# Three fused layers on one core: weight conversion in fewer steps, paced differently, and decay tables widened on GpSimd

## The chip, the cores and the metric

The kernel runs on one NeuronCore of one Trainium2 chip. The metric is the device time of one execution in microseconds. Engines are named PE (TensorE matmul), DVE (VectorE), ACT (ScalarE), POOL (GpSimd) and SP (SyncE, whose queue issues the DMAs).

## What is computed

Three layers follow one another, each on the output of the one before:

```python
# 1. retention: q, k, v are (batch 4, heads 8, seq 576, dim 64)
ret = (q @ k.T / 8) * Dmat          # Dmat[i, j] = gamma_h ** (i - j) for i >= j, else 0
x = ret @ v                         # reshaped to (2304, 512)
# 2. feed-forward, w_in (512, 2048), w_out (2048, 512)
h = x @ w_in
x = (h * clip(h + 3, 0, 6) / 6) @ w_out
# 3. feed-forward, w_in (512, 1024), w_out (1024, 512)
h = x @ w_in
solu = h * softmax(h)
ln = (solu - mean) / sqrt(var + 1e-6) * g_ln
out = ln @ w_out
```

The four weight matrices arrive as 64-bit floats (each as two 32-bit words). The retention inputs arrive as 32-bit floats.

## The kernel before, in words

**Matmuls in three passes.** For the two feed-forward layers every operand is held as a sum of two parts, hi and lo, that PE's fp32r format can hold. A product is three matmuls: hi by hi, hi by lo, lo by hi (`mlp_h`, `mlp_x2`, `mm_h2`, `mm_out`).

**Weight conversion.** `Weights.split` turns one half-tile of 128 x 512 64-bit weights (512 KB, tile `wraw`, two buffers) into hi and lo. It builds the 32-bit value from the two words. First ACT scales the upper word read as a float (L119, into `wz`). Then DVE shifts it left by three bits (L122, into `wt`), puts the sign bit back (L123), masks out the exponent (L124), multiplies the lower word by it (L125) and adds both (L128). Then ACT rounds the sum to hi (L130) and DVE subtracts hi to get lo (L132; every third time on POOL). L125 is the last reader of `wraw`: the next load into that buffer waits for it. There are 48 conversions: 12 during the retention, 20 in the first feed-forward layer, 16 for the last layer's weights (these have lines L134 and L135 for half of them).

**Pacing.** The retention runs over 16 pairs of heads (`attention`), three steps `s` to a pair. PE's program order for pair n is: scores s(n), chunk states u(n), values xp(n-1), last scores z(n), values from the states xp(n-1). DVE does the masked copy `st` (L334), the states (L350), `st4` (L361) and the scaled result `xa` (L387). From step W_FROM = 5 on, two of three steps also call `wq.step()`, which converts one half-tile: steps 5, 6, 8, 9, 11, 12, 14, 15, 17, 18, 20, 21. From pair A_FROM = 5 on, each step also issues two pieces of the first feed-forward layer (`mlp_a`). That layer's second matmuls (`mlp_x2`) begin at step 27 and need conversions 6 to 11.

**Queues.** All bulk DMAs are issued in program order by SP. An instruction in SP's queue that waits (a `wraw` load for its buffer, say) holds up everything behind it. A scheduler sets the order on each engine. What is given below is the order that it made.

**Decay tables.** One DMA (`decay`, 128 x 524) brings four 128-column tables and twelve columns of factors. ACT copies the tables into four tables of 576 columns (`tab_sb`, L442, 20 copies), which `xa` reads.

Of the kernel before, what the change touches and what calls it, by code (L numbers as in the profile page):

```python
# [26 lines left out]
N_DEC = 128 * (H // 2) + H + H // 2  # L27
# [9 lines left out]
W_LOAD = 4  # L37
W_FROM = 5
# [20 lines left out]
def retention_hardswish_solu_kernel(ctx, tc, kt, qt, kn, vt, w1, w2i, w2o, gln, decay, out):  # L59
# [29 lines left out]
    class Weights:  # L89
# [22 lines left out]
        def split(self, raw, w, scale=None, done=None):  # L112


            z = p0.tile([128, 512], F32, tag="wz", bufs=2, name="wz")
            t = p0.tile([128, 512], I32, tag="wt", bufs=2, name="wt")
            zi, f = z.bitcast(I32), t.bitcast(F32)

            first = se.activation(out=z, in_=raw[:, :, 1].bitcast(F32), func=ACTF.Copy, scale=2.0 ** -112)  # L119
# [168 lines left out]
    def load_pair(pr):  # L288
# [50 lines left out]
    def chunk_states(pr):  # L339
# [379 lines left out]
```

## Time and profile before

| | |
|---|---|
| median of 3 runs | 715.96 us (714.98 to 716.06) |
| profiled execution, its own time | 715.41 us |
| its span in the trace | 713.7 us |
| PE busy | 680.6 us, 95% |
| DVE busy | 441.9 us, 62% |
| ACT busy | 307.2 us, 43% |
| POOL busy | 249.1 us, 35% |
| mean granted TensorE clock | 0.978 |

The first two lines are device times. The span is the stretch that the trace covers; the profiled execution took 1.7 us more than its span. PE's share of busy time is an average over stages with different limits, so it doesn't say by itself which engine a stage waits for. A table by stretches does: each of its rows gives, for a stretch of the span, each engine's busy time with its count of instructions, the granted clock, and how busy the DMA engines were.

### The profile page before, as it was taken

How to read it: one execution, taken by the hardware profiler on the slowest of the kernel's cores; microseconds unless marked ns; L12 is line 12 of the kernel's file. 1: busy time of each engine (PE TensorE's matmuls, PEld its weight loads, DVE VectorE, ACT ScalarE, POOL GpSimd, SP SyncE). 2: the span in 40 equal slices, each digit the busy share in tenths (PEclk: the TensorE clock that was granted, in tenths of full speed). 3: DMA queues.
4: the chain of work that ended last, by engine and by line, in shares of the span. 5: the costliest groups of instructions: out<-in, count | busy, mean ns of one | idle time of the engine just before them, and what ended most of it. 6: DMA issues, size and time to landing. Idle time of an engine off the chain costs nothing.

```text
span 713.7 us, 10518 instructions
## 1 busy us (share of the span) xinstructions
PE 680.6 (95%) x3968; PEld 560.5 (79%) x3968; DVE 441.9 (62%) x673; ACT 307.2 (43%) x536; POOL 249.1 (35%) x233
## 2 busy tenths in 40 slices
PE   7577899999998999999999999999999999999998
PEld 5565677788886997778778888889988888888887
DVE  3899943240496387925777785411178877776780
ACT  4335442342544435433524524413247555454453
POOL 2233341240533133353633502422236633331333
PEclk8789999999999999999999999999999999999999
DMA  9676666113151533315568365013655643233233
GB/s 332 230 227 206 202 191 197 58 45 74 59 192 45 178 110 100 116 56 181 179 198 272 125 228 180 29 45 130 251 166 133 148 89 74 69 80 74 60 82 81
DMA packets 76259, 97.96 MB, mean 137 GB/s; under 512 B 42672, under 2 KB 44976, under 8 KB 75184
## 3 DMA queue, kind: packets, MB, share of 16 engines
q1 hardware_dynamic: 76208, 97.29, 45.1%
q8 instruction: 31, 0.51, 0.3%
q14 instruction: 20, 0.16, 0.1%
HBM read 63.71 MB, written 24.12 MB: 123 GB/s over the span
## 4 chain that ended last, share of the span: by engine, by line
PE 70%; DVE 12%; DMA 7%; issue 5%; ACT 3%; POOL 1%; SPq 0%; DVEq 0%; POOLq 0%; ACTq 0%
PE h L189 17%; PE x L210 16%; PE o L625 14%; PE h L559 14%; DMA wraw<-in_w_dram 6%; PE acc L210 4%; PE xp L286 3%; DVE wt L122 2%; DVE wt L123 2%; DVE wz L125 2%; ACT wz L119 1%; DVE wt L128 1%; PE s L286 1%; DVE wz L124 1%; PE u L286 1%
## 5 line engine op out<-in xcount | busy, mean ns | idle before, releaser
L204 POOL TENSOR_TENSOR g<-gf,g 128x512 fp32r<-128x512 f32 (+1 forms) x80 | 101.4, 1269 | 218.4 <-ACT g L203 194.7
L210 PE MATMUL x<-g,w 128*128 128x512 f32 x648 | 154.6, 393 | 3.0 <-DVE gf L200 1.5
L210 PEld LDWEIGHTS x<-g,w 128*128 128x128 f32 x648 | 120.0, 188 | 31.1 <-DVE gf L200 2.2
L189 PE MATMUL h<-xb,w 128*128 128x512 f32 (+1 forms) x600 | 137.3, 366 | 3.9 <-ACT w L130 2.4
L189 PEld LDWEIGHTS h<-xb,w 128*128 128x128 f32 x600 | 101.8, 193 | 22.4 <-ACT w L130 2.8
L200 DVE SCALAR_TENSOR_TENSOR gf<-r,h 128x512 f32<-128x512 f32 (+1 forms) x80 | 50.3, 629 | 87.2 <-ACT r L199 70.0
L559 PE MATMUL h<-w2i,x2b 128*128 128x512 f32 x432 | 102.0, 389 | 0.0
L625 PE MATMUL o<-w2o,lt 128*128 128x512 f32 (+1 forms) x456 | 101.0, 378 | 0.0
L625 PEld LDWEIGHTS o<-w2o,lt 128*128 128x128 f32 x456 | 82.5, 188 | 16.0
L559 PEld LDWEIGHTS h<-w2i,x2b 128*128 128x128 f32 x432 | 80.6, 188 | 16.3
L189 PE MATMUL h<-xB,w 128*128 128x512 f32 x360 | 82.4, 389 | 0.0
L180 POOL TENSOR_TENSOR lt<-lT,lt 128x512 fp32r<-128x512 f32 x36 | 46.3, 1305 | 93.8 <-ACT lt L179 93.8
L189 PEld LDWEIGHTS h<-xB,w 128*128 128x128 f32 x360 | 67.6, 188 | 14.0
L203 ACT ACTIVATE g<-gf 128x512 fp32r<-128x512 f32 (+1 forms) x80 | 46.9, 587 | 64.3 <-DVE gf L200 64.2
L199 ACT ACTIVATE r<-h,half 128x512 f32<-128x512 f32 (+1 forms) x80 | 50.7, 636 | 40.1 <-PE h L189 39.8
L210 PE MATMUL acc<-g,w 128*128 128x256 f32 (+1 forms) x312 | 63.8, 328 | 0.7 <-ACT x2p L262 0.5
L122 DVE TENSOR_SCALAR wt<-wz 128x512 int32<-128x512 int32 x48 | 33.4, 695 | 39.4 <-ACT wz L119 39.0
L210 PEld LDWEIGHTS acc<-g,w 128*128 128x128 f32 x312 | 50.5, 191 | 8.3 <-POOL g L204 1.0
L180 POOL TENSOR_TENSOR xb<-xa,xb 128x512 fp32r<-128x512 f32 (+7 forms) x32 | 29.1, 927 | 59.9 <-ACT xb L179 59.9
L128 DVE TENSOR_TENSOR wt<-wt,wz 128x512 f32<-128x512 f32 x48 | 44.8, 934 | 0.6
L119 ACT ACTIVATE wz<-wraw 128x512 f32<-128x512 f32 x48 | 31.5, 662 | 26.7 <-DMA wraw<-in_w_dram 21.4
L130 ACT ACTIVATE w<-wt 128x512 fp32r<-128x512 f32 x32 | 20.2, 631 | 45.0 <-DVE wt L128 45.0
(77 smaller groups left out, 744.1 us busy)
## 6 DMA issues: line engine op xcount, KB each, us to landing
wraw<-in_w_dram SPq DMA_DIRECT2D x32, 512.0 KB, 4.2
rv<-in_vt_dram SPq DMA_DIRECT2D x16, 320.0 KB, 4.7
x2l<-x2s SPq DMA_DIRECT2D x18, 256.0 KB, 5.0
out_dram<-osb SPq DMA_DIRECT2D x17, 256.0 KB, 2.0
x2s<-x2p SPq DMA_DIRECT2D x16, 256.0 KB, 3.7
wraw<-in_w2i_dram SPq DMA_DIRECT2D x8, 512.0 KB, 5.7
w2is<-wsi SPq DMA_DIRECT2D x8, 512.0 KB, 4.2
wraw<-in_w2o_dram SPq DMA_DIRECT2D x8, 512.0 KB, 4.8
```

Of the source, the lines that this page charges most:

```text
L119: first = se.activation(out=z, in_=raw[:, :, 1].bitcast(F32), func=ACTF.Copy, scale=2.0 ** -112)
L122: ve.tensor_scalar(out=t, in0=zi, scalar1=3, scalar2=None, op0=ALU.logical_shift_left)
L128: ve.tensor_tensor(out=f, in0=f, in1=z, op=ALU.add)
L180: ge.tensor_tensor(out=x[:, 1, c], in0=src, in1=f32(x[:, 0, c]), op=ALU.subtract)
L189: nc.tensor.matmul(hp, w1t[ff][:, a, c], xb[t, p][:, b, :n], start=(p == 0 and i == 0), stop=(p == NP - 1 and i == 2),)
L199: se.activation(out=r, in_=hp, func=ACTF.Relu, scale=1.0 / 6.0, bias=half)
L200: ve.scalar_tensor_tensor(out=gf, in0=r, scalar=1.0, in1=hp, op0=ALU.min, op1=ALU.mult)
L203: se.activation(out=g[ff][:, 0], in_=gf, func=ACTF.Copy)
L204: ge.tensor_tensor(out=g[ff][:, 1], in0=gf, in1=f32(g[ff][:, 0]), op=ALU.subtract)
L210: nc.tensor.matmul(acc, w1t[ff][:, a, c], g[:, b], start=(first and i == 0), stop=(last and i == 2))
L559: nc.tensor.matmul(h[:, m], x[:, a, c], w[:, b, m * 512:(m + 1) * 512], start=(d == 0 and j == 0), stop=(d == NP - 1 and j == 2),)
L625: nc.tensor.matmul(op, lt[:, a, ff % 4], w[:, b, c:c + n], start=(ff == 0 and j == 0), stop=(ff == NFF2 - 1 and j == 2),)
```

## The change

Three edits.

**Conversion.** L119's copy becomes a two-slope activation (`Prelu`): negative inputs are multiplied by a further 2**32, which shifts their exponent so that the left shift by three brings the sign bit out by itself. The instruction that put the sign back is gone. hi is now made by ACT from the shifted upper word alone, right after the shift, and no longer from the sum. lo is the sum (now written to `wz`) less hi.

**Pacing.** The weight loads begin at step 2 and the conversions at step 4. Up to pair 4 there is one conversion per pair, from pair 5 on two of three steps: steps 4, 7, 10, 13, 16, 17, 19, 20, 22, 23, 25, 26.

**Tables.** The twelve factor columns are a small DMA of their own, now first in SP's queue. The tables (`place`, 128 x 512) follow after pair 0's loads, and POOL widens them in eight copies; ACT's twenty copies are gone.

```diff
-W_LOAD = 4
-W_FROM = 5
+W_LOAD = 2
+W_FROM = 4
...
-            first = se.activation(out=z, in_=raw[:, :, 1].bitcast(F32), func=ACTF.Copy, scale=2.0 ** -112)
+            first = se.activation(
+                out=z, in_=raw[:, :, 1].bitcast(F32), func=ACTF.Prelu, scale=2.0 ** -112, alpha=2.0 ** 32
+            )
...
             ve.tensor_scalar(out=t, in0=zi, scalar1=3, scalar2=None, op0=ALU.logical_shift_left)
-            ve.scalar_tensor_tensor(out=t, in0=zi, scalar=-2 ** 31, in1=t, op0=ALU.bitwise_and, op1=ALU.bitwise_or)
+            se.activation(out=w[:, 0], in_=f, func=ACTF.Copy, scale=1.0 if scale is None else scale)
             ve.tensor_scalar(out=zi, in0=t, scalar1=-2 ** 23, scalar2=None, op0=ALU.bitwise_and)
...
-            ve.tensor_tensor(out=f, in0=f, in1=z, op=ALU.add)
+            ve.tensor_tensor(out=z, in0=f, in1=z, op=ALU.add)
             if scale is None:
-                se.activation(out=w[:, 0], in_=f, func=ACTF.Copy)
                 eng = ge if self.at % 3 == 2 else ve
-                eng.tensor_tensor(out=w[:, 1], in0=f, in1=f32(w[:, 0]), op=ALU.subtract)
+                eng.tensor_tensor(out=w[:, 1], in0=z, in1=f32(w[:, 0]), op=ALU.subtract)
...
-        if pr == 0:
-            nc.sync.dma_start(out=decay_sb, in_=decay)
...
+        if pr == 0:
+            nc.sync.dma_start(out=place_sb, in_=place)
...
+    nc.sync.dma_start(out=decay_sb, in_=decay)
     for pr in range(EARLY):
         load_pair(pr)
...
-        for c in CHUNKS:
-            se.activation(out=tab_sb[p][:, c], in_=decay_sb[:, 128 * p:128 * p + c.stop - c.start], func=ACTF.Copy)
+        ge.tensor_copy(
+            out=tab_sb[p][:, :512].rearrange("p (c q) -> p c q", q=128),
+            in_=place_sb[:, p].unsqueeze(1).to_broadcast([128, 4, 128]),
+        )
+        ge.tensor_copy(out=tab_sb[p][:, 512:], in_=place_sb[:, p, :64])
...
-        if s >= W_FROM and (s - W_FROM) % 3 != 2:
+        if s >= W_FROM and (s - W_FROM) % 3 < (1 if pr < A_FROM else 2):
             wq.step()
```

**What moves on DVE, in pairs 1 and 2.** Names are tile and number; `wt`, `wz` and `w1_0` belong to the first conversion. Before, from the result of pair 0 on:

```order
L387 TENSOR_TENSOR xa0_279<-xp0_251,tab_sb0_96 128x576
L122 TENSOR_SCALAR wt_292<-wz_291 128x512
L123 SCALAR_TENSOR_TENSOR wt_292<-wz_291,wt_292 128x512
L124 TENSOR_SCALAR wz_291<-wt_292 128x512
L334 TENSOR_TENSOR st2_302<-s2_303,mask_100 128x1024
L125 SCALAR_TENSOR_TENSOR wz_291<-wraw_260,wz_291 128x512
L350 SCALAR_TENSOR_TENSOR state2_337<-state2_337,decay_sb_95,u2_336 128x64
L128 TENSOR_TENSOR wt_292<-wt_292,wz_291 128x512
L350 SCALAR_TENSOR_TENSOR state2_337<-state2_337,decay_sb_95,u2_336 128x64 x2
L132 TENSOR_TENSOR w1_0_176<-wt_292,w1_0_176 128x512
```

The same place now, with the new line numbers (L126 the shift, L128 the mask, L129 the product, L132 the sum, L135 lo):

```order
L353 SCALAR_TENSOR_TENSOR state1_232<-state1_232,decay_sb_95,u1_231 128x64 x2
L126 TENSOR_SCALAR wt_257<-wz_256 128x512
L353 SCALAR_TENSOR_TENSOR state1_232<-state1_232,decay_sb_95,u1_231 128x64
L128 TENSOR_SCALAR wz_256<-wt_257 128x512
L129 SCALAR_TENSOR_TENSOR wz_256<-wraw_205,wz_256 128x512
L364 TENSOR_TENSOR st41_266<-z1_265,mask4_102 128x64
L132 TENSOR_TENSOR wz_256<-wt_257,wz_256 128x512
L135 TENSOR_TENSOR w1_0_166<-wz_256,w1_0_166 128x512
L390 TENSOR_TENSOR xa0_280<-xp0_245,tab_sb0_97 128x576
L337 TENSOR_TENSOR st2_291<-s2_292,mask_101 128x1024
```

The first conversion moved from behind `xa0` to ahead of it, into pair 1. One conversion then stands in each pair up to pair 4, always ended before that pair's `xa`.

**What moves in SP's queue.** After pair 2's last load, before:

```order
L309 DMA raw2_126<-in_kn_dram 128x512
L300 DMA rk3_229<-in_kt_dram 128x576
L301 DMA rq3_230<-in_qt_dram 128x576
L308 DMA rv3_234<-in_vt_dram 128x640
L309 DMA rn3_231<-in_kn_dram 128x512
L102 DMA wraw_260<-in_w1_dram 128x1024
```

And now:

```order
L310 DMA raw2_128<-in_kn_dram 128x512
L102 DMA wraw_205<-in_w1_dram 128x1024
L102 DMA wraw_207<-in_w1_dram 128x1024
L303 DMA rk3_223<-in_kt_dram 128x576
L304 DMA rq3_224<-in_qt_dram 128x576
L309 DMA rv3_228<-in_vt_dram 128x640
```

The first two weight loads now stand ahead of pair 3's four loads.

**What moves on PE, in pair 9**, where the second matmuls of the first feed-forward layer begin (`x2_0_0`; `w1_3` and `w1_5` are the weights of conversions 9 and 11). Before:

```order
L210 MATMUL x2_0_0_1047<-g0_3_900,w1_3_179 128x512 x3
L286 MATMUL z9_1094<-rq9_860,rk9_859 64x64 x2
...
L210 MATMUL x2_0_0_1047<-g0_4_955,w1_4_180 128x512 x3
L210 MATMUL x2_0_0_1047<-g0_5_1033,w1_5_181 128x512 x3
L286 MATMUL s10_1127<-rq10_962,rk10_961 128x128 x8
L210 MATMUL x2_0_1_1137<-g0_0_658,w1_0_176 128x512 x3
```

And now:

```order
L212 MATMUL x2_0_0_1025<-g0_3_849,w1_3_169 128x512
L212 MATMUL x2_0_1_1115<-g0_0_607,w1_0_166 128x512 x3
...
L212 MATMUL x2_0_0_1025<-g0_3_849,w1_3_169 128x512 x2
...
L212 MATMUL x2_0_0_1025<-g0_5_1011,w1_5_171 128x512
L212 MATMUL x2_0_1_1115<-g0_3_849,w1_3_169 128x512 x2
L212 MATMUL x2_0_1_1115<-g0_4_915,w1_4_170 128x512 x3
...
L212 MATMUL x2_0_0_1025<-g0_5_1011,w1_5_171 128x512 x2
L289 MATMUL s10_1105<-rq10_922,rk10_921 128x128 x8
```

The matmuls that need lo of conversions 9 and 11 moved back, behind pieces of `x2_0_1`; the rest of PE's order up to pair 9 is as before.

## Rows read from the trace of the kernel before

**Rows 1.** The page: span, busy times, and PE's granted clock in 40 slices.

```profile
span 713.7 us, 10518 instructions
...
PE 680.6 (95%) x3968; PEld 560.5 (79%) x3968; DVE 441.9 (62%) x673; ACT 307.2 (43%) x536; POOL 249.1 (35%) x233
...
PEclk8789999999999999999999999999999999999999
```

**Rows 2.** Windows, each from one pair's scores on PE to the next's.

```profile
core 0: us, PE busy (x) PEld busy (x) DVE busy (x) ACT busy (x) POOL busy (x), PEclk, DMA share, GB/s
22.36:33.00 10.64, 6.82 (x72) 5.76 (x73) 10.20 (x19) 4.16 (x9) 2.19 (x2) 0.68 0.60 199
33.00:43.75 10.75, 6.55 (x73) 5.53 (x73) 9.81 (x17) 4.15 (x9) 3.45 (x3) 0.68 0.65 210
...
68.37:76.89 8.52, 8.52 (x92) 6.52 (x91) 8.06 (x12) 3.86 (x8) 4.67 (x5) 1.00 0.74 237
...
98.08:106.59 8.51, 8.51 (x93) 6.52 (x92) 3.05 (x6) 2.57 (x7) 1.57 (x3) 1.00 0.65 198
```

**Rows 3.** Groups of DVE, 22.36 to 89.51 us: busy us, mean ns.

```profile
L128 DVE TENSOR_TENSOR wt<-wt,wz 128x512 f32<-128x512 f32 x12 | 10.1, 842 | 0.1
L123 DVE SCALAR_TENSOR_TENSOR wt<-wz,wt 128x512 int32<-128x512 int32 x11 | 9.5, 863 | 0.2
L125 DVE SCALAR_TENSOR_TENSOR wz<-wraw,wz 128x512 f32<-128x512 uint32 x12 | 9.0, 753 | 0.1
L122 DVE TENSOR_SCALAR wt<-wz 128x512 int32<-128x512 int32 x11 | 8.6, 779 | 1.5 <-ACT wz L119 1.2
L334 DVE TENSOR_TENSOR st<-s,mask 128x1024 f32<-128x1024 f32 x6 | 7.3, 1212 | 0.0
L132 DVE TENSOR_TENSOR w<-wt,w 128x512 fp32r<-128x512 f32 x8 | 6.1, 760 | 1.4 <-ACT w L130 1.3
L350 DVE SCALAR_TENSOR_TENSOR state<-state,decay_sb,u 128x64 f32<-128x64 f32 x21 | 5.7, 272 | 0.1
L124 DVE TENSOR_SCALAR wz<-wt 128x512 int32<-128x512 int32 x11 | 4.6, 416 | 0.1
L387 DVE TENSOR_TENSOR xa<-xp,tab_sb 128x576 f32<-128x576 f32 x6 | 4.5, 748 | 0.0
L200 DVE SCALAR_TENSOR_TENSOR gf<-r,h 128x512 f32<-128x512 f32 x5 | 3.4, 676 | 0.0
L361 DVE TENSOR_TENSOR st<-z,mask 128x64 f32<-128x64 f32 x6 | 1.3, 214 | 0.0
```

**Rows 4.** Timeline of the start: start us, us, engine, line, instruction.

```profile
8.62 0.33 SPq L300 DMA_DIRECT2D rk<-in_kt_dram  x1
...
16.84 0.76 DVE L387 TENSOR_TENSOR xa<-xp,tab_sb 128x576 f32<-128x576 f32 x1 [0.67 <-PE xp L286]
```

**Rows 5.** DMA, issued 8 to 9 us: KB each, us to landing.

```profile
rk<-in_kt_dram SPq DMA_DIRECT2D x1, 288.0 KB, 6.0
```

**Rows 6.** DMA, 0 to 30 us: rate in 40 slices of 0.75 us.

```profile
GB/s 0 0 117 344 305 257 268 354 346 392 397 410 407 405 396 391 393 396 397 385 403 401 426 376 324 393 390 407 394 368 143 40 235 328 147 55 251 227 255 98
```

**Rows 7.** Waits of PE, 190 to 380 us: total, times, longest.

```profile
PE h L189 <- ACT w L130: 2.4, 1, 2.4
```

**Rows 8.** Windows where PE stands idle after the retention.

```profile
217.00:228.00 11.00, 9.21 (x37) 6.86 (x38) 8.74 (x13) 5.46 (x10) 3.01 (x3) 1.00 0.15 54
302.00:308.00 6.00, 3.62 (x9) 2.69 (x9) 5.22 (x10) 2.58 (x5) 1.65 (x2) 0.73 0.00 0
347.00:354.00 7.00, 5.71 (x26) 4.39 (x24) 5.65 (x7) 4.08 (x8) 4.65 (x4) 1.00 0.64 207
```

**Rows 9.** Groups by shape, whole span: copies on ACT, work on POOL.

```profile
L204 POOL TENSOR_TENSOR g<-gf,g 128x512 fp32r<-128x512 f32 x64 | 88.2, 1381 | 172.5 <-ACT g L203 166.0 <-PE h L189 3.8 <-issue 2.7
...
L119 ACT ACTIVATE wz<-wraw 128x512 f32<-128x512 f32 x48 | 31.5, 662 | 26.7 <-DMA wraw<-in_w_dram 21.4 <-DMA wraw<-in_w2i_dram 3.7 <-DMA wraw<-in_w2o_dram 1.3
...
L428 POOL TENSOR_SCALAR_AFFINE_SELECT mask<-mask 128x1024 f32<-128x1024 f32 x1 | 1.1, 1092 | 0.0
```

More of the change, by code (lines that the diff above doesn't have):

```diff
@@ L26 @@
 GAMMA = [1.0 - 2.0 ** (-5 - h) for h in range(H)]
-N_DEC = 128 * (H // 2) + H + H // 2
+N_DEC = H + H // 2
 NPAIR = NH // 2
@@ L58, in retention_hardswish_solu_kernel @@
 @with_exitstack
-def retention_hardswish_solu_kernel(ctx, tc, kt, qt, kn, vt, w1, w2i, w2o, gln, decay, out):
+def retention_hardswish_solu_kernel(ctx, tc, kt, qt, kn, vt, w1, w2i, w2o, gln, decay, place, out):
     nc = tc.nc
@@ L127, in split @@
             )
-            ve.tensor_tensor(out=f, in0=f, in1=z, op=ALU.add)
+            ve.tensor_tensor(out=z, in0=f, in1=z, op=ALU.add)
             if scale is None:
-                se.activation(out=w[:, 0], in_=f, func=ACTF.Copy)
                 eng = ge if self.at % 3 == 2 else ve
-                eng.tensor_tensor(out=w[:, 1], in0=f, in1=f32(w[:, 0]), op=ALU.subtract)
+                eng.tensor_tensor(out=w[:, 1], in0=z, in1=f32(w[:, 0]), op=ALU.subtract)
             else:
-                se.activation(out=w[:, 0], in_=f, func=ACTF.Copy, scale=scale)
                 ve.scalar_tensor_tensor(
-                    out=w[:, 1], in0=f, scalar=scale, in1=f32(w[:, 0]), op0=ALU.mult, op1=ALU.subtract
+                    out=w[:, 1], in0=z, scalar=scale, in1=f32(w[:, 0]), op0=ALU.mult, op1=ALU.subtract
                 )
@@ L273, in retention_hardswish_solu_kernel @@
     decay_sb = pa.tile([128, N_DEC], F32, name="decay_sb")
+    place_sb = pa.tile([128, NP, 128], F32, name="place_sb")
     tab_sb = [pa.tile([128, S], F32, name=f"tab_sb{p}") for p in range(NP)]
@@ L318, in prep @@
         for h in range(2):
-            head = 128 * NP + 2 * (pr % NP) + h
+            head = 2 * (pr % NP) + h
             se.activation(
@@ L346, in chunk_states @@
                 mm_a(up[HEADS[h], c], rn[:, c, HEADS[h]], v[:, h, c], start=(c == 0), stop=(c == 3))
-        at = 128 * NP + H + pr % NP
+        at = H + pr % NP
         se.activation(out=state[:, 0], in_=up[:, 0], func=ACTF.Copy)
@@ L670, in retention_hardswish_solu_kernel @@
     pb.release()
-_INS = ["kt", "qt", "kn", "vt", "w1", "w2i", "w2o", "gln", "decay"]
+_INS = ["kt", "qt", "kn", "vt", "w1", "w2i", "w2o", "gln", "decay", "place"]
 def kernel(**inputs):
@@ L700 @@
     gamma = np.asarray(GAMMA)
-    place = np.arange(128, dtype=np.float64)
-    tab = np.repeat((gamma[:, None] ** (place + 128) / np.sqrt(D)).reshape(NP, 2, 128), 64, axis=1).transpose(1, 0, 2)
-    over = gamma[None, :] ** -place[:, None]
+    b = np.arange(128, dtype=np.float64)
+    tab = np.repeat((gamma[:, None] ** (b + 128) / np.sqrt(D)).reshape(NP, 2, 128), 64, axis=1).transpose(1, 0, 2)
+    over = gamma[None, :] ** -b[:, None]
     step = np.repeat((gamma ** 128).reshape(NP, 2), 64, axis=1).T
-    decay = np.concatenate([tab.reshape(128, NP * 128), over, step], axis=1).astype(np.float32)
-    host = dict(kt=kt, qt=qt, kn=kn, vt=vt, w1=w1, w2i=w2i, w2o=w2o, gln=gln, decay=decay)
+    place = tab.reshape(128, NP, 128).astype(np.float32)
+    decay = np.concatenate([over, step], axis=1).astype(np.float32)
+    host = dict(kt=kt, qt=qt, kn=kn, vt=vt, w1=w1, w2i=w2i, w2o=w2o, gln=gln, decay=decay, place=place)
     nc = _bacc.Bacc("TRN2", target_bir_lowering=False, num_devices=1)
```

## The prediction

> **What bounds the kernel now.** I read the page first. PE is busy for 680.6 of 713.7 us, so on the whole PE is the bound, but its granted clock is under full in the first five slices, up to some 90 us, and at full speed nearly everywhere after [rows 1]. So the first 90 us are a stage of their own. Windows cut from one pair's scores on PE to the next pair's show what limits it [rows 2]. In pairs 3 and 4 (22.36 to 43.75 us) a pair takes 10.7 us: DVE is busy for 10.20 and 9.81 of it, PE for only 6.8 and 6.6, at 0.68 of its clock. DVE is the bound there. In the window from 98.08 us, where no weights are converted, a pair takes 8.51 us, PE is busy for all of it at full clock, and DVE for 3.05. Between these lie pairs 5 to 9, where both engines are near full: from 68.37 us DVE is busy for 8.06 of 8.52 us and PE doesn't stand still.
>
> What fills DVE is seen in its groups from 22.36 to 89.51 us [rows 3]. One pair's own work is one `st` (1.21), three state steps (0.27 each), one `st4` (0.21) and one `xa` (0.75): 2.99 us. One conversion is L122 0.78, L123 0.86, L124 0.42, L125 0.75, L128 0.84 and two thirds of a 0.76 us L132 (the others are POOL's): 4.16 us on the mean. With two conversions in a pair that is all of the 10.7 us.
>
> After the retention PE is full, but for a few places. Three windows hold the largest: PE idles for 11.00 - 9.21 = 1.8 us from 217 us, 6.00 - 3.62 = 2.4 from 302 us (there at 0.73 of the clock too) and 7.00 - 5.71 = 1.3 from 347 us [rows 8]. The 2.4 us are a wait for hi of a weight (L130) [rows 7].
>
> **The retention: three stretches, against the profiled execution.**
>
> *To pair 3's scores* (before: 22.36). The first conversion now stands on DVE ahead of pair 0's `xa`, and DVE runs in order, so `xa` waits for the first weight load to land. That load takes the place of pair 3's first load, which was issued at 8.62 [rows 4] and took 6.0 us for 288 KB [rows 5], so landed at 14.6. Loads arrive there at some 390 GB/s [rows 6]: 288 KB are 0.75 us, so what was ahead had landed at 13.9, and 512 KB more land at 15.2. Then come ACT's 0.66 [rows 9] and on DVE L122, L124, L125, L128, L132, a state step and `st4`. By the means of [rows 3] that is 0.78 + 0.42 + 0.75 + 0.84 + 0.76 + 0.27 + 0.21 = 4.0 us, so `xa` begins near 19.9, against 16.84 [rows 4]. It ends at 20.6, and PE needs about half of a pair's 6.6 to 6.8 us after it before it comes to s(3): 23 to 24. So this stretch **loses** 0.5 to 1.5 us; I take 0.7. What is bought is that this conversion is done by then, while before it stood in pair 2. ACT's tables are gone and factors arrive sooner, but pair 0 can't use that, since its `xa` is what waits.
>
> *Pairs 3 and 4* (before: 21.4 us). One conversion per pair in place of two, each without L123: 4.16 - 0.86 = 3.30 us. DVE needs 2.99 + 3.30 = 6.3 us per pair. From the pair's own windows, which hold fewer collisions, a conversion costs (10.0 - 3.0) / 2 = 3.5, less 0.7 to 0.9 is 2.7, and a pair 5.7. PE's 6.6 to 6.8 us per pair at 0.68 of its clock is then as long, and would be shorter at full clock. I take 6.5: 13.0 us, a gain of **8.4** (7.8 to 10).
>
> *From pair 5's scores to pair 11's* (before: 43.75 to 106.59, 62.8 us). PE's work on these six pairs is the same pieces as before. At the 8.51 us of the last window it is 51.1 us, which is the floor. DVE has eight conversions left, 8 x 3.30 = 26.4, six pairs' own work, 17.9, and six of the first layer's `gf` at 0.68, 4.1: 48.4 us. That is 95% of the floor, the same share as in the window from 68.37 us, in which PE didn't stand still. But it isn't spread evenly: the conversions end with the one at step 26, and `x2_0_0` on PE needs it from step 27 on. By the sum, DVE gets to that conversion's last step at 36.1 + 45.4 = 81.5 and POOL's part ends 1.4 us later [rows 9], near 83, when PE, unhindered, has done five pairs at 36.1 + 42.6 = 78.7. So PE waits there for up to 4 us less what it has of other pieces. I take 3.5 us for this and other stops: 54.6, a gain of **8.2** (4 to 11.8).
>
> From pair 11 on PE is the bound and its order is that of before, so what has been won is kept: 0.7 - 8.4 - 8.2 = **-15.9 us**.
>
> **The conversions after the retention.** Each has one DVE instruction less, and hi no longer waits for L123, L124, L125 and L128 (2.9 us by [rows 3]); lo comes L123 and ACT's rounding sooner, some 1.5 us. `wraw` is released 0.86 us sooner, so the next load starts sooner. The 2.4 us wait for hi [rows 7] goes, with most of its clock dip; of the 3.1 us of the other two windows, which are waits behind a DVE that conversions fill (6.86 of 11 us, 5.65 of 7), I take a third to a half. POOL's lo now keeps `wz`, and an ACT instruction waits for it where a DVE one did. Gain **3.5 us** (1 to 6). The 16 conversions of the last layer stand beside a full PE and bring nothing.
>
> **Edits costed at nothing.** *The two-slope activation*: the trace has none. The nearest row is the same instruction with a copy, 0.66 us [rows 9]; if it took twice that, ACT would have 48 x 0.66 = 32 us more, at 43% busy, and each conversion would start its DVE part 0.66 us later, behind DVE's other work. I take 0.66. The instruction list of the changed kernel has one table load, as before. The Trainium skill's page "ScalarE: Activation LUTs", in its section "What ACT_TABLE_LOAD costs", speaks against mixing functions: a switch between table sets costs about 2.66 us. By that rule 96 switches would be an estimated 255 us; with a single load in the list the rule has nothing to act on here, and the sum goes without it.
>
> *The tables on POOL*: four copies of 128 x 512 and four of 128 x 64. The nearest rows are the select over 1024 columns, 1.09, and a two-operand subtraction over 512, 1.38 [rows 9]: for all eight between 2.5 and 7.8 us (the short ones at an eighth to a half of the long). The tables land with pair 0's loads, some 6 us before the first weights do, and the first `xa` reads only the first one, near 20 us. POOL's next job comes after that `xa`. Even 7.8 us are hidden; without that cover it would be 1.4 us once.
>
> **Sum.** 715.4 - 15.9 - 3.5 = **696.0 us** for the profiled execution. The median of the runs, 715.96, is 0.5 us above it; I keep 696.0. Under 0.2% is about what a measurement of this kernel can't tell from no change.
>
> **The rivals.**
>
> *The loads become the bound.* A pair brings 1.18 MB, a weight 0.52, and 0.29 go out: 2.0 MB in 6.5 us is 308 GB/s, and with two weights 2.5 MB in 8.5 to 9 us some 290. For it: from 22 to 77 us the DMA engines gave 199 to 237 GB/s at a share of 0.60 to 0.74, some 320 at a full share [rows 2], and SP issues in order, so a weight load that waits for its buffer holds up a pair's loads. Against it: at the start they gave 390 to 410 [rows 6], and pairs 3 and 4 are issued early. At 240 GB/s a pair takes 8.3 us and a pair with two weights 10.4. The second stretch then gains 4.8 and the third (four such pairs and two of 8.5) 4.2, so the sum is 0.7 - 4.8 - 4.2 - 3.5 = -11.8: **703 to 704**.
>
> *Weights come too late* (the other side). The last conversion moved from step 21 to 26, one step ahead of its use, and PE runs in order: everything behind `x2_0_0` stands. The rest of the retention starts later than before if PE gets past this place after the old 98.08. By the sum it does so near 83 to 85, so DVE would have to fall 13 us behind: eight conversions at 4.9 in place of 3.30 us, as when POOL's subtractions held up most of their steps. Then all of the gain ahead is lost, and at 1 us past the point, with nothing won later because the same collisions go on: **717**.
>
> *More is won.* Third stretch at its floor and all idle places gone: 0.7 - 10 - 11.8 - 6 = -27: **688**.
>
> *Little is won*: DVE's freed time is refilled by the conversions that move back, and only the missing L123 counts, 12 x 0.86 in the retention, less the 0.7, and 1 us later: 715.4 - 10.6, **705**, and up to 714 where part of that is lost too.
>
> **How the numbers follow.** Forecast, 690 to 701: 0.64. Loads: 0.18. Little won, 704 to 714: 0.05. More won, below 690: 0.07. No change within 0.2%: 0.02. Late weights, slower: 0.04. So faster 0.94, same 0.02, slower 0.04. The range of 689.5 to 706 leaves out most of the last cases at both ends, under 2 in 10.
>
> **What would show it.** Pair 0's `xa` at 19 to 21 us behind a conversion; s(5) near 36 and s(11) near 91 (before: 43.75, 106.59); pairs 3 and 4 at 6 to 7 us each with one conversion; DVE over 90% busy from there to 82 us; a wait of PE on a weight of conversion 9 or 11 near 80 us; no 2.4 us wait for hi later. I am wrong if pairs 3 and 4 take over 8 us with DVE idle (loads), if PE stands for 10 us before `x2_0_0` (late weights), or if ACT shows more than one table load.

## The result

The changed kernel takes **692.12 us** (median of four runs, 691.34 to 695.16), before 716.01 (714.98 to 716.47): a ratio of 0.9676 by the means of the runs (the medians give 0.9666), with an interval of 0.9645 to 0.9707. The forecast was 696.0. Run again later, beside other kernels, it took 690.49 us, a ratio of 0.9633 (0.9619 to 0.9648), so the gain is 24 to 27 us. The profiled execution took 691.34 us.

The page of the changed kernel, its answer to [rows 1]:

```profile
span 689.3 us, 10482 instructions
PE 671.5 (97%) x3968; PEld 555.8 (81%) x3968; DVE 406.2 (59%) x625; ACT 303.7 (44%) x516; POOL 249.6 (36%) x241
PEclk8999999999999999999999999999999999999999
```

DVE has 48 instructions less, one for each conversion, and PE is busy for 9.1 us less with the same 3968 matmuls. Matmuls take longer at a lower granted clock (23 of them in 6.92 busy us at 0.76, 32 in 7.00 us at 1.00, in rows further below), and the mean granted clock rose from 0.978 to 0.993. So much of this is clock won back: the row of the clock reads 8 in the first slice alone.

The windows of the changed kernel from one pair's scores to the next's, as in [rows 2] (pairs 3 to 9, and 11):

```profile
core 0: us, PE busy (x) PEld busy (x) DVE busy (x) ACT busy (x) POOL busy (x), PEclk, DMA share, GB/s
22.35:31.28 8.93, 5.67 (x76) 4.75 (x72) 6.98 (x16) 4.20 (x10) 2.02 (x3) 0.84 0.81 266
31.28:35.23 3.95, 3.95 (x74) 3.59 (x72) 3.90 (x10) 1.99 (x6) 3.02 (x3) 0.94 0.85 241
35.23:44.43 9.20, 8.80 (x94) 6.52 (x90) 8.57 (x17) 5.33 (x12) 1.76 (x2) 1.00 0.99 306
44.43:52.94 8.51, 8.51 (x92) 6.52 (x91) 6.32 (x12) 4.83 (x11) 4.24 (x4) 1.00 0.87 273
52.94:61.70 8.76, 8.60 (x92) 6.52 (x91) 8.55 (x12) 4.63 (x10) 4.70 (x5) 1.00 0.79 252
61.70:73.09 11.39, 9.13 (x92) 6.79 (x91) 10.73 (x22) 7.41 (x16) 5.88 (x6) 1.00 0.76 232
73.09:86.84 13.75, 13.62 (x113) 9.66 (x112) 12.21 (x21) 5.61 (x12) 6.08 (x6) 1.00 0.69 218
...
91.11:99.62 8.51, 8.51 (x92) 6.52 (x91) 3.32 (x7) 3.02 (x7) 1.60 (x3) 1.00 0.75 206
```

Pair 3 begins at the same time as before (22.35 and 22.36). Pairs 3 and 4 together take 12.88 us in place of 21.4; pair 11 begins at 91.11 in place of 106.59. In pairs 5 and 9 DVE is busy for 93% and 89%, and PE for 96% and 99%.

Where the 24.4 us between the two spans went is found with one more cut. From the last pair's scores (156.63 before, 141.20 after) to the first matmul of the last hidden layer (504.48, 480.18), the stage behind the retention, the windows of before and of after are:

```profile
156.63:504.48 347.85, 340.21 (x1704) 284.11 (x1701) 203.28 (x297) 139.44 (x242) 121.39 (x95) 1.00 0.41 133
```

```profile
141.20:480.18 338.98, 336.25 (x1705) 283.57 (x1702) 177.76 (x261) 139.56 (x242) 120.55 (x95) 1.00 0.42 136
```

So the retention won 15.4 us, and the stage behind it 8.9 (the expectations below say 9.0): PE's idle time there fell from 7.64 to 2.73 us, by 4.9, and the busy time of the same matmuls by 4.0. The last stage takes 209.2 and 209.1 us.

Beside the wait for hi [rows 7], the longest waits of PE in this stage were, before (total, times, longest):

```profile
PE x L210 <- DVE gf L200: 1.5, 2, 0.8
PE x L210 <- ACT g L203: 1.5, 1, 1.5
PE h L189 <- ACT x2p L262: 1.0, 1, 1.0
```

and now all that is left is

```profile
PE h L191 <- ACT x2p L264: 1.6, 1, 1.6
PE x L212 <- POOL g L206: 1.2, 1, 1.2
```

(`gf` and `g` are made between a layer's two matmuls, and `x2p` is ACT's copy of a result.) Of the 4.0 us of busy time 1.7 are clock: before, the granted clock was 0.76 over the 7 us from 304 (0.24 of 7 us lost), behind the wait for hi (its row stands further below). The rest goes with the number of stops, 8 before and 2 now. The record of one matmul lasts 0.39 us, while the next begins 0.21 us after it where PE is full, so a stop is longer than the idle time that the trace gives it. Around a wait for `gf`, before:

```profile
222.64 0.39 PE L189 MATMUL h<-xb,w 128*128 128x512 f32 x1
223.88 1.43 PE L210 MATMUL x<-g,w 128*128 128x512 f32 x5 [0.84 <-DVE gf L200]
```

The matmul behind the stop begins 1.24 us after the one ahead of it, where 0.84 of idle time and 0.21 would be 1.05, and the five take 1.43 us, where at full rate they take 1.24: 0.4 us beside the idle time. At some 0.3 to 0.4 us each, six stops fewer are an estimated 2 us, near the 2.3 that the clock leaves.

### The profile page after: what moved, and what is told of

Read it like the earlier page. It is cut to its first block, busy times and chain, and to the rows that moved or that the text cites. A ratio compares the mean times of both kernels' runs of the same rounds, so it can differ in the third digit from the quotient of the medians.

```text
span 689.3 us, 10482 instructions
## 1 busy us (share of the span) xinstructions
PE 671.5 (97%) x3968; PEld 555.8 (81%) x3968; DVE 406.2 (59%) x625; ACT 303.7 (44%) x516; POOL 249.6 (36%) x241
## 4 chain that ended last, share of the span: by engine, by line
PE 76%; DMA 8%; DVE 7%; issue 3%; POOL 2%; ACT 1%; SPq 0%; DVEq 0%; POOLq 0%; ACTq 0%
PE h L191 19%; PE x L212 18%; PE o L632 14%; PE h L566 14%; PE acc L212 7%; DMA xs<-xa 2%; PE xp L289 2%; DVE wz L129 2%; POOL g L206 2%; DVE wz L132 1%; DMA rn<-in_kn_dram 1%; DMA wraw<-in_w_dram 1%; DVE gf L202 1%; PE s L289 1%; DVE wt L126 1%
## 5 line engine op out<-in xcount | busy, mean ns | idle before, releaser
L191 PE MATMUL h<-xb,w 128*128 128x512 f32 (+1 forms) x600 | 134.0, 360 | 1.7 <-ACT x2p L264 1.6
L191 PEld LDWEIGHTS h<-xb,w 128*128 128x128 f32 x600 | 99.8, 189 | 18.9 <-ACT x2p L264 2.4
L632 PEld LDWEIGHTS o<-w2o,lt 128*128 128x128 f32 x456 | 82.5, 188 | 15.9
L212 PE MATMUL acc<-g,w 128*128 128x256 f32 (+1 forms) x312 | 62.3, 323 | 0.0
L126 DVE TENSOR_SCALAR wt<-wz 128x512 int32<-128x512 int32 x48 | 33.5, 700 | 43.7 <-ACT wz L121 43.5
L129 DVE SCALAR_TENSOR_TENSOR wz<-wraw,wz 128x512 f32<-128x512 uint32 x48 | 39.8, 830 | 0.8
L132 DVE TENSOR_TENSOR wz<-wt,wz 128x512 f32<-128x512 f32 x48 | 36.1, 753 | 0.9
```

What stands on the lines that cost most here:

```text
L129: ve.scalar_tensor_tensor(out=z, in0=raw[:, :, 0].bitcast(U32), scalar=2.0 ** -52, in1=z, op0=ALU.mult, op1=ALU.mult)
L132: ve.tensor_tensor(out=z, in0=f, in1=z, op=ALU.add)
L191: nc.tensor.matmul(hp, w1t[ff][:, a, c], xb[t, p][:, b, :n], start=(p == 0 and i == 0), stop=(p == NP - 1 and i == 2),)
L212: nc.tensor.matmul(acc, w1t[ff][:, a, c], g[:, b], start=(first and i == 0), stop=(last and i == 2))
L632: nc.tensor.matmul(op, lt[:, a, ff % 4], w[:, b, c:c + n], start=(ff == 0 and j == 0), stop=(ff == NFF2 - 1 and j == 2),)
```

## The experiments

Twelve runs followed, one of them the changed kernel again. Since before has 715.96 to 717.53 us beside the different sets, ratios are compared, not times. "Last pair" is the start of the last pair's scores; "stage behind" runs from there to the first matmul of the last hidden layer. Both are read from one profiled execution of each kernel. With two buffers for `xa`, pieces of the last pairs stand elsewhere in PE's order, so those two columns stay empty for such kernels.

| kernel | median us | ratio to before, 95% | last pair | stage behind |
|---|---|---|---|---|
| before | 715.96 to 717.53 | | 156.63 | 347.85 |
| changed | 692.12 | 0.9676 (0.9645 to 0.9707) | 141.20 | 338.98 |
| changed, again | 690.49 | 0.9633 (0.9619 to 0.9648) | 140.25 | 339.56 |
| tables alone | 715.32 | 0.9989 (0.9975 to 1.0004) | 156.13 | 348.19 |
| conversion alone | 703.97 | 0.9828 (0.9806 to 0.9850) | 152.73 | 340.08 |
| pacing alone | 707.09 | 0.9871 (0.9844 to 0.9897) | 146.96 | 349.53 |
| conversion and pacing | 691.21 | 0.9651 (0.9629 to 0.9674) | 140.69 | 338.37 |
| hi from the sum | 696.60 | 0.9718 (0.9693 to 0.9744) | 141.98 | 343.69 |
| sign step back, hi early | 707.37 | 0.9863 (0.9845 to 0.9881) | 147.50 | 349.74 |
| sign step back, hi behind it | 709.42 | 0.9879 (0.9843 to 0.9916) | 147.44 | 352.72 |
| two `xa` | 689.63 | 0.9614 (0.9591 to 0.9637) | | |
| two `xa`, dense from pair 4 | 695.45 | 0.9689 (0.9661 to 0.9717) | | |
| two `xa`, dense from pair 6 | 689.10 | 0.9613 (0.9599 to 0.9628) | | |
| two `xa`, tables on ACT | 688.80 | 0.9617 (0.9593 to 0.9642) | | |

### Each edit alone

**Tables alone** is the kernel before with `place_sb` and the copies on POOL, as the change's diff shows them.

> Before, with the tables edit alone: the decay tables are widened by GpSimd. Theory: ScalarE's table copies lie ahead of nothing that sets the end, so the time stays within 0.2% of before: 715 to 717 us. Rival (the copies held up the first conversion on ScalarE and so the start): 1 to 2 us faster, 714 us.

Measured: the interval holds 1. The edit is worth nothing that can be measured, and **conversion and pacing** without it confirm this from the other side.

> Before, with conversion and pacing edits, tables left on ScalarE. Theory: the changed kernel's time within 0.2%: 691.5 to 694 us; the start may lose up to 0.7 us. Rival (GpSimd's tables free ScalarE in the first 20 us, on which xa0 hangs): 694 to 696 us.

Measured: 0.9651, between the two measurements of the changed kernel. The copies on POOL lie where nothing waits: in the timeline of the changed kernel they run from 8.39 to 11.38 us, and the first `xa`, which reads them, begins at 19.37.

**Pacing alone** is the kernel before with

```diff
-W_LOAD = 4
-W_FROM = 5
+W_LOAD = 2
+W_FROM = 4
-        if s >= W_FROM and (s - W_FROM) % 3 != 2:
+        if s >= W_FROM and (s - W_FROM) % 3 < (1 if pr < A_FROM else 2):
```

> Before, with the pacing edit alone: the same five VectorE steps for each conversion, one conversion in the early pairs and the rest spread to later pairs. Theory: retention gains what lies free in the pairs that TensorE bounds (VectorE 3.05 us busy of 8.5), about 6 to 9 us; after retention nothing is gained, since hi still waits for the sign step: 707 to 710 us. Rival (the later gain of 9.0 us comes from the state in which pacing leaves the queues): 698 to 701 us. Rival on the other side (conversions with the sign step come too late for convolutions 9 and 11): 716 us or more.

Measured: 0.9871. The last pair starts 9.7 us sooner, and the stage behind gains nothing (it is 1.7 us longer): near the theory's numbers (6 to 9 us, and none). What it can't do is shown by its waits of PE in the retention from 23 to 100 us (total, times, longest), where the five-step conversion still holds up `xa` and a weight of the second layer:

```profile
PE xp L286 <- DVE xa L387: 7.9, 6, 2.7
PE x L210 <- ACT w L130: 1.6, 1, 1.6
```

**Conversion alone** is the kernel before with the edit in `split`:

```diff
-            first = se.activation(out=z, in_=raw[:, :, 1].bitcast(F32), func=ACTF.Copy, scale=2.0 ** -112)
+            first = se.activation(
+                out=z, in_=raw[:, :, 1].bitcast(F32), func=ACTF.Prelu, scale=2.0 ** -112, alpha=2.0 ** 32
+            )
...
-            ve.scalar_tensor_tensor(out=t, in0=zi, scalar=-2 ** 31, in1=t, op0=ALU.bitwise_and, op1=ALU.bitwise_or)
+            se.activation(out=w[:, 0], in_=f, func=ACTF.Copy, scale=1.0 if scale is None else scale)
...
-                se.activation(out=w[:, 0], in_=f, func=ACTF.Copy)
```

> Before, with the conversion edit alone (two-slope activation, no sign step, hi from the word), old pacing and old tables. Theory (retention is bound by VectorE's work per pair, and the later gain of 9.0 us belongs to hi being early): each of the five retention pairs that carry two conversions loses 2 x 0.75 us of VectorE work, so about 1.5 us each, 6 to 8 us in all, and the 9.0 us after retention come whole: 699 to 702 us. Rival A (the pacing gave most of the retention's 15.4 us and the later gain both, because weights and loads queue otherwise): 708 to 712 us. Rival B (the conversion alone gave everything): 692 to 694 us.

Measured: 0.9828, some 4 us short of the theory. The stage behind gains most of what there is (7.8 of 8.9 us), but the retention only 3.9 us where 6 to 8 were expected. Its windows of pairs 3 and 4 show that DVE isn't full any more, and PE isn't either:

```profile
23.11:32.99 9.88, 6.05 (x73) 5.23 (x73) 8.29 (x17) 4.19 (x9) 1.75 (x2) 0.65 0.58 178
32.99:43.28 10.29, 6.09 (x72) 5.27 (x72) 8.57 (x16) 4.19 (x9) 3.26 (x3) 0.67 0.69 219
```

Its timeline in pair 4 shows the new stop:

```profile
37.70 0.75 DVE L389 TENSOR_TENSOR xa<-xp,tab_sb 128x576 f32<-128x576 f32 x1
38.49 0.77 ACT L181 ACTIVATE xb<-xa 128x512 fp32r<-128x512 f32 x2 [3.65 <-DVE xa L389]
39.17 0.65 ACT L121 ACTIVATE wz<-wraw 128x512 f32<-128x512 f32 x1
39.85 0.91 DVE L126 TENSOR_SCALAR wt<-wz 128x512 int32<-128x512 int32 x1 [1.40 <-ACT wz L121]
```

ACT runs in order. It stands 3.65 us at `xb`, waiting for DVE's `xa`, and the next conversion's first step, which is behind `xb`, can't start; so DVE has nothing to do for 1.40 us once `xa` is done. From pair 3 to pair 6 DVE stands 5.6 us in four such waits. The freed time became a wait in a chain DVE, ACT, DVE. With pacing added the same wait is 1.4 us, once, in these pairs (**conversion and pacing**); that it is the slack around `xa` that breaks the chain is argued and not shown by itself. The two edits together win 15.9 us in the retention, some 2 more than 3.9 and 9.7; the start of the last pair differed by 1 us between two executions of the changed kernel.

### What of the conversion edit counts

The edit does two things: it takes a step of DVE away, and it makes hi right behind the first step, where before it stood behind the fifth. Three kernels take them apart, all with the changed pacing and tables.

**Hi from the sum** keeps the four steps and makes hi three of them later (mask, product and sum; the expectation counts two):

```diff
-            se.activation(out=w[:, 0], in_=f, func=ACTF.Copy, scale=1.0 if scale is None else scale)
             ve.tensor_scalar(out=zi, in0=t, scalar1=-2 ** 23, scalar2=None, op0=ALU.bitwise_and)
             ve.scalar_tensor_tensor(
                 out=z, in0=raw[:, :, 0].bitcast(U32), scalar=2.0 ** -52, in1=z, op0=ALU.mult, op1=ALU.mult
             )
             ve.tensor_tensor(out=z, in0=f, in1=z, op=ALU.add)
+            se.activation(out=w[:, 0], in_=z, func=ACTF.Copy, scale=1.0 if scale is None else scale)
```

> The changed kernel with VectorE's four steps, but hi rounded from the finished sum, two VectorE steps later, instead of from the upper word; the values of hi differ in the last place where that rounding differs. Theory (the 9.0 us behind retention come from hi being early): retention as in the changed kernel within 1 us, and 5 to 9 us lost behind it: 697 to 701 us. Rival A (they come from the VectorE step that is gone, which shortens every wait for a weight whatever hi is made of): 692 to 694 us. Rival B (hi's lateness also holds up retention's ScalarE work): 702 us or more.

Measured: 0.9718. Its last pair is 0.8 to 1.7 us behind the changed kernel's, and it loses 4.1 to 4.7 us behind the retention, about half of what was to be explained. That lies between the theory and rival A. How it loses them is nearer to rival B, behind the retention in place of in it: none of PE's waits there (5.7 us) is for a weight. They are for `x2p`, `g` and `gf`, the longest

```profile
PE acc L212 <- ACT x2p L264: 1.9, 1, 1.9
```

and ACT, which works in order, stands longer at hi. Its waits there in this kernel and in the changed one:

```profile
ACT w L132 <- DVE wz L131: 16.2, 12, 2.7
```

```profile
ACT w L127 <- DVE wt L126: 9.6, 12, 1.8
```

So what a late hi costs here is seen in the work that stands behind it on ACT.

**Sign step back, hi behind it** puts the removed instruction back where it stood, ahead of hi; the activation has written the sign already, so it writes what is there:

```diff
+            ve.scalar_tensor_tensor(out=t, in0=zi, scalar=-2 ** 31, in1=t, op0=ALU.bitwise_and, op1=ALU.bitwise_or)
             se.activation(out=w[:, 0], in_=f, func=ACTF.Copy, scale=1.0 if scale is None else scale)
```

> The changed kernel with VectorE's sign step put back (it writes what is there already, so the product is the same) and hi made behind it; pacing and tables stay changed. Theory (the four-step chain and pacing give the gain, not the activation's form): as with pacing and tables alone, 705 to 708 us, with the last retention pair at 146 to 148 us (141.20 in the changed kernel) and the first hidden-layer matmul of the last stage 348 to 350 us behind that (339.0). Rival (part of the gain is from something else that the conversion edit moves, such as the order of ScalarE's work): 698 to 702 us.

Measured: 0.9879, near the ratio of pacing alone (0.9871), though 709.42 us is over the 705 to 708 expected; the rival is out. The last pair is at 147.44. The stage behind took 352.72 us, over the 348 to 350 expected, in a profiled execution (711.01 us) that was near the longest of its runs (705.27 to 711.02).

**Sign step back, hi early** has the same work on DVE, but hi is made ahead of it:

```diff
             se.activation(out=w[:, 0], in_=f, func=ACTF.Copy, scale=1.0 if scale is None else scale)
-            ve.tensor_scalar(out=zi, in0=t, scalar1=-2 ** 23, scalar2=None, op0=ALU.bitwise_and)
+            t2 = p0.tile([128, 512], I32, tag="wt2", bufs=1, name="wt2")
+            ve.scalar_tensor_tensor(out=t2, in0=zi, scalar=-2 ** 31, in1=t, op0=ALU.bitwise_and, op1=ALU.bitwise_or)
+            ve.tensor_scalar(out=zi, in0=t2, scalar1=-2 ** 23, scalar2=None, op0=ALU.bitwise_and)
```

> The changed kernel with the sign step put back as a step of its own tile, while hi stays early (it is made from the upper word ahead of the sign step). Theory (the gain of the conversion edit is VectorE work taken out of a chain that TensorE waits for, in retention and behind it, and hi's earliness is worth only what the kernel with hi from the sum lost, 4.7 us behind retention): retention's last pair at 146 to 148 us, 344 to 349 us from there to the first matmul of the last stage, 703 to 707 us. Rival (the sign step costs only by holding up hi): last pair at 141 to 143 us, 339 to 341 us behind it, 692 to 695 us.

Measured: 0.9863, not to be told from the kernel with hi behind the step. The last pair is 6.3 to 7.3 us late and the stage behind 10.2 to 10.8 longer than in the changed kernel, so the stage is a little over the theory's range; the rival is out. Its waits of PE from 190 to 320 us show why early hi didn't help (total, times, longest):

```profile
PE h L193 <- DVE w L137: 3.3, 1, 3.3
PE x L214 <- DVE gf L204: 3.1, 1, 3.1
```

and its windows around the first of these, at 298.08 us:

```profile
291.00:298.00 7.00, 3.76 (x17) 2.79 (x15) 6.15 (x11) 2.99 (x5) 1.59 (x1) 1.00 0.26 75
298.00:305.00 7.00, 6.92 (x23) 5.60 (x24) 2.93 (x6) 2.88 (x5) 5.25 (x4) 0.76 0.00 1
305.00:312.00 7.00, 7.00 (x32) 5.81 (x31) 0.69 (x1) 2.37 (x4) 4.77 (x5) 1.00 0.43 111
```

It is the same weight for whose hi PE waits before [rows 7], two matmuls further on. Here hi is there, and PE waits 3.3 us for lo (`w`, L137) in its place, which DVE makes last. DVE is busy for 6.15 of the 7 us ahead, and as soon as it has nothing more to convert PE is full. Before looks the same there:

```profile
297.00:304.00 7.00, 5.22 (x22) 3.98 (x22) 6.96 (x12) 2.65 (x6) 1.56 (x1) 1.00 0.22 75
304.00:311.00 7.00, 6.39 (x21) 5.14 (x22) 3.40 (x6) 3.97 (x7) 4.65 (x4) 0.76 0.00 0
```

DVE had 6.96 of 7.00 us. The answer in the changed kernel, with PE full while the same conversions end:

```profile
272.00:279.00 7.00, 7.00 (x33) 5.79 (x32) 6.90 (x10) 2.54 (x5) 3.07 (x2) 1.00 0.43 150
279.00:285.00 6.00, 6.00 (x28) 4.99 (x27) 5.60 (x9) 3.29 (x6) 2.23 (x2) 1.00 0.00 0
```

So in a burst of conversions DVE's time is what PE waits for. Four kinds with the new pacing stand side by side in the stage behind: with the step and hi late 349.53 us (pacing alone), with the step and hi early 349.74, without the step and hi late 343.69, without it and hi early 338.98 and 339.56. The missing step is worth 5.8 us with hi late, more than half of the gain; hi's early start is worth 4 to 5 us when the step is gone, and nothing measurable when it is there.

### The new wait, and the pacing's place

The changed kernel's waits of PE in the retention, 22.35 to 100 us:

```profile
PE xp L289 <- DVE xa L390: 4.3, 3, 3.0
PE u L289 <- ACT v L323: 1.2, 1, 1.2
```

The longest is behind a wait of DVE in pair 3 that was not there before. The timeline:

```profile
20.33 0.95 SPq L396 DMA_DIRECT2D xs<-xa  x2
...
26.97 0.76 DVE L390 TENSOR_TENSOR xa<-xp,tab_sb 128x576 f32<-128x576 f32 x1 [1.74 <-DMA xs<-xa]
```

`xa` has one buffer, and the transfer that reads the last one, issued at 20.33, hadn't ended: its 256 KB took 6.3 us to land. **Two `xa`** takes that away:

```diff
-        xa = pa.tile([128, S], F32, tag="xa", bufs=1, name=f"xa{pr}")
+        xa = pa.tile([128, S], F32, tag="xa", bufs=2, name=f"xa{pr}")
```

> The changed kernel with two buffers for xa, so that VectorE needn't wait for the transfer that reads the last one. Theory (the waits of VectorE for that transfer, 2.9 us in three places of retention, lie on the path of the pairs that VectorE bounds): 1 to 3 us faster than the changed kernel, 689.1 to 691.1 us. Rival (the weight conversions behind it take the place of the wait, and the pair ends when they end): within 0.2% of the changed kernel, 691 to 693.5 us.

Measured: 0.9614, against 0.9633 for the changed kernel in the later set. The wait is gone, and pairs 3 and 4 take 10.91 us in place of 12.88, at full clock:

```profile
21.83:27.61 5.78, 4.35 (x77) 3.64 (x73) 5.61 (x12) 2.98 (x7) 1.76 (x3) 1.00 0.96 316
27.61:32.74 5.13, 4.41 (x76) 3.66 (x73) 5.06 (x12) 3.02 (x8) 3.18 (x4) 1.00 0.82 246
```

In the profiled executions it is 2.3 us ahead (689.06 against 691.34), inside the theory's range, but the intervals overlap, so the total doesn't settle it.

**Two `xa`, dense from pair 4** and **from pair 6** move the pair from which two of three slots convert; the first reads

```diff
-        if s >= W_FROM and (s - W_FROM) % 3 < (1 if pr < A_FROM else 2):
+        if s >= W_FROM and (s - W_FROM) % 3 < (1 if pr < A_FROM - 1 else 2):
```

and the second has `A_FROM + 1` in its place.

> As the kernel with two buffers for xa, and the denser rate of weight conversions (two of three slots) begins one pair earlier, at pair 4. Theory (the changed kernel's pairs 8 and 9, 11.39 and 13.75 us for 9.13 and 13.62 us of TensorE, wait for work that could lie in pairs 5 and 6, where VectorE has room): 1 to 2 us faster than with the two buffers alone, 688 to 690 us. Rival (the work moved forward collides there, and TensorE waits in pairs 5 and 6 in place of 8): 0 to 3 us slower than with the two buffers alone, 690 to 694 us.

Measured: 0.9689, 5.8 us slower than two `xa` alone and clear of it; more than the rival gave. The profiled execution (692.77) is the quickest of its four runs, so its trace shows only 3.7 of the 5.8 us. Its pairs 7 and 8 take 10.89 and 11.81 us with DVE full and PE at 8.9 and 9.1:

```profile
52.88:63.77 10.89, 8.86 (x92) 6.63 (x91) 10.75 (x18) 6.02 (x12) 4.47 (x4) 1.00 0.83 257
63.77:75.58 11.81, 9.11 (x91) 6.78 (x90) 11.20 (x22) 7.05 (x15) 6.66 (x6) 1.00 0.73 223
```

> Two buffers for xa, and the denser rate of conversions begins at pair 6, one pair later than in the changed kernel. Theory (weights that come later are waited for: the second block's hidden matmuls run ahead of the first conversions of the other weights): TensorE waits for a weight in pairs 8 to 10 or just behind retention, 1 to 6 us slower than with two buffers alone, 690.5 to 696 us. Rival (pairs 5 and 6 have VectorE room to win, as they lost when the rate began at pair 4): 0 to 2 us faster, 687.5 to 689.6 us.

Measured: 0.9613, the same as two `xa`. The weights do come late now, as the theory said, but for less: PE waits 1.0 us for hi (L127) and 0.7 for lo (L135) between 22 and 100 us. Pair 8 takes 8.50 us in place of 10.48, and the first matmul of the last hidden layer comes at 478.64 us, 0.5 later than with two `xa` alone. So, moved by one pair, the place of the dense rate has an edge on the early side and is flat on the late one.

> Two buffers for xa, with the conversion and pacing edits but the decay tables left on ScalarE as before. Theory (the tables edit is worth nothing, 0.1% in either direction in the runs so far): the same as with two buffers alone within 0.2%, a ratio of 0.960 to 0.963 to before. Rival (the tables edit costs 0.9 us, as the kernel without it was 691.21 us against 692.12): 688 to 689 us, ratio 0.958 to 0.960.

This is the kernel with two `xa` and the tables' copies on ACT as before. Measured: 0.9617, the theory: the tables edit counts for nothing here either.

> The changed kernel once more, unaltered, so that the kernels of this set stand beside it under like conditions. Both theories: its ratio to before between 0.9645 and 0.9707, as measured first.

Measured: 0.9633, just under the first interval. By the intervals no kernel tried is shown to beat the changed one. In the same set, though, all four runs of two `xa` with the dense rate from pair 6 (688.45 to 689.64) lie under all four of the changed kernel (689.80 to 691.20): 1.4 us, or 0.2%.

## Why the prediction was right, and where not

*To pair 3's scores.* Forecast a loss of 0.7 us, measured none. The mechanism was there: the first conversion stands ahead of pair 0's `xa`, and ACT waits for the load (start, us, idle before):

```profile
15.54 0.67 ACT L121 ACTIVATE wz<-wraw 128x512 f32<-128x512 f32 x1 [1.39 <-DMA wraw<-in_w_dram]
```

```profile
19.37 0.75 DVE L390 TENSOR_TENSOR xa<-xp,tab_sb 128x576 f32<-128x576 f32 x1
```

The forecast had the load at 15.2 and `xa` at 19.9. The `xa` began 2.5 us later than before [rows 4], and pair 3's scores no later. Before, they waited for `st` of pair 2, which stood on DVE behind three steps of the first conversion (start, us, idle before):

```profile
22.36 1.16 PE L286 MATMUL s<-rq,rk 64*128 64x128 f32 x16 [1.84 <-DVE st L334]
```

Now that conversion is done by then, and `st` follows `xa` at once. The forecast counted half a pair of PE's work behind `xa` (3.3 us), and it was 2.2.

*Pairs 3 and 4.* Forecast 13.0 us, measured 12.88, but not as drawn: 6.5 and 6.5 were meant, 8.93 and 3.95 came. Pair 3 holds the wait for the transfer that reads `xa`, which the prediction didn't have; pair 4 then ran with PE full. That the sum came out within 0.1 us is luck. With that wait gone, two `xa` shows 10.91.

*From pair 5's scores to pair 11's.* Forecast 54.6, measured 55.88. The wait for the weights of the second layer near 80 us did not come (pair 9: PE 13.62 of 13.75); the stops were in pair 8 instead, 2.3 us, for `v` and `xa`. The size held within 1.3 us, the place did not, so this too is in part luck. DVE was busy for 74% of pair 6, 98% of pair 7 and 89% to 94% of pairs 5, 8 and 9, 90% of the stretch from 35.23 to 86.84 us, where over 90% was forecast. A conversion took 3.4 us of DVE where the sum had 3.30. Some of its means rose and others fell: lo took 0.95 us in place of 0.76 in [rows 3], the sum 0.79 in place of 0.84, in the groups of DVE from 22.35 to 86.84 us:

```profile
L132 DVE TENSOR_TENSOR wz<-wt,wz 128x512 f32<-128x512 f32 x11 | 8.7, 794 | 0.1
...
L135 DVE TENSOR_TENSOR w<-wz,w 128x512 fp32r<-128x512 f32 x7 | 6.6, 948 | 0.3
```

Retention in all: 15.4 us, forecast 15.9.

*The conversions after the retention* are the term that was mis-sized: 8.9 us, forecast 3.5 with 1 to 6. The step in question is "The 2.4 us wait for hi [rows 7] goes, with most of its clock dip; of the 3.1 us of the other two windows, which are waits behind a DVE that conversions fill (6.86 of 11 us, 5.65 of 7), I take a third to a half." Two things were wrong in it. First, 2.4 and a third to a half of 3.1 are already 3.4 to 4.0 us, so the dip was named and put at nothing. PE's waits fell by 4.9 us, somewhat more than that, and its busy time by 4.0, for which the sum has no term: 1.7 of clock and some 2 around the stops. At the one place, before did 43 matmuls in the 14 us from 297 to 311, and the changed kernel 61 in the 13 us from 272: at its 0.21 us each, 43 are 9.2 us, so 4.8 were lost there, half of it the wait and 1.7 the clock. Second, the wait of 2.4 us was put at hi, which the change makes sooner, when it was DVE, full in each burst: with hi as early as in the changed kernel and the step put back, 10.2 to 10.8 us are lost; with hi late and the step gone, 4.1 to 4.7. DVE was also fuller than the prediction read: in the window from 217 us it is busy for 8.74 of 11 us, and 6.86 is the weight loads' figure (PEld) [rows 8].

The two losses are not terms of a sum (15 us by these, while pacing alone is 10.0 to 10.6 from the changed kernel): hi early is worth something only where the step is gone. What stays open is why the three kernels with the step and the new pacing took longer there than before, by 1.7 to 4.9 us (349.53, 349.74 and 352.72 against 347.85).

*The edits costed at nothing.* The two-slope activation took what the copy took (0.66 us in [rows 9]), with a single table load in the trace. The Trainium skill's page "ScalarE: Activation LUTs", section "What ACT_TABLE_LOAD costs", which prices a switch to a different table set, had nothing to act on. The one load took 1.283 us, and no run here shows a switch.

```profile
L121 ACT ACTIVATE wz<-wraw 128x512 f32<-128x512 f32 x48 | 31.6, 664 | 33.8 <-DMA wraw<-in_w_dram 20.0 <-DVE wso L137 3.5 <-DMA wraw<-in_w2i_dram 2.9
L323 ACT ACT_TABLE_LOAD x1 | 1.3, 1283 | 6.6 <-DMA rv<-in_vt_dram 6.6
```

The copies on POOL took 0.61 and 0.24 us, 3.4 for all eight, within 2.5 to 7.8.

*The rivals.* Loads: they did become nearly full (a share of 0.99 at 306 GB/s in pair 5), but PE was busy for 8.80 of 9.20 us there (the rival was worked out at 240 GB/s). Pair 3 did show the sign that was set for this rival, over 8 us (8.93) with DVE idle for 1.95; what DVE waited for was a transfer out that took 6.3 us to land among the loads, and not a load. Pair 4, at 3.95 us, made up for it. Late weights on the other side: the kernel with the dense rate one pair later shows the waits begin, at 1.7 us. Little won: pacing and conversion alone each win less than together, and conversion alone shows the refilling that this rival meant, in the retention: 3.9 us.

## What to carry to other kernels

An engine that is busy for 60% of the span can still be what the bound engine waits for, if its work comes in bursts: look at short windows ahead of each wait, and if the engine that makes the missing operand is full there, take instructions out of the burst first; making one result sooner helped here only once that was done. Price a wait of PE by the wait, by the clock behind it and by what is lost around each stop; here the last two together were four fifths of the first. And two edits that take the same engine's load off, one by less work and one by spreading it, won some 2 us more together than apart, where a chain over two engines in order had refilled what one of them freed.

## What the runs showed of the hardware

The clock: behind a wait of 3.3 us, with PE busy for 3.76 of the 7 us ahead, the granted clock was 0.76 over the next 7 us, a mean of its levels of 1.2 and 2.4 GHz, and PE did 23 matmuls there in place of 32 (the windows of the kernel with the sign step back and hi early); in the changed kernel, where PE was busy for 5.43 of 7 us with one wait of 1.57, it was 1.00 there and in the 7 us behind:

```profile
201.00:208.00 7.00, 5.43 (x24) 4.43 (x24) 5.42 (x9) 3.68 (x7) 2.67 (x2) 1.00 0.10 37
208.00:215.00 7.00, 7.00 (x32) 5.80 (x31) 1.18 (x2) 2.27 (x4) 3.84 (x3) 1.00 0.00 0
```

DVE beside POOL: a DVE step with one input, `L130`, took 1.40 us in place of 0.42 (its next one, at 292.76 us), as the timeline of the kernel with the sign step back and hi early shows:

```profile
287.30 1.67 POOL L137 TENSOR_TENSOR w<-wz,w 128x512 fp32r<-128x512 f32 x1 [0.63 <-DVE wz L134]
287.86 1.40 DVE L130 TENSOR_SCALAR wz<-wt 128x512 int32<-128x512 int32 x1
```

POOL's subtraction spans 287.30 to 288.97 and DVE's step ends 0.29 us after it. The Trainium skill's page "SBUF — State Buffer", section "SBUF: two separate sides", says that the two share a pair of ports, held by whichever starts first for its whole instruction, when VectorE's is in a two-port mode or has two SBUF inputs; the trace agrees in the time, 1.40 us for 0.42, and doesn't show the mode. In the changed kernel no 128x512 step of a conversion took DVE over 0.76 us unless POOL worked beside it, and beside POOL they took up to 1.79. So lo on POOL takes work off DVE and holds DVE up at once.
